# A three-stage kernel on one Trainium2 core: the float64 weights of its first MoE converted without limits, with two VectorE instructions a tile where there were three

## The chip, the cores and the metric

The kernel runs on one core of one Trainium2 chip. The metric is the device time of one execution in microseconds (us). Five engines work side by side, each through its own queue in order: TensorE (PE, with its weight loads as PEld), VectorE (DVE), ScalarE (ACT), GpSimd (POOL) and SyncE (SP), which here issues the loads and stores to HBM.

## The reference, cut to what matters

Attention over a window of 128 positions feeds a dense layer ("first MoE"), and that feeds a layer of eight experts of which each token takes two. The inputs `moe_w_in` and `moe_w_out` arrive as float64.

```python
attn_out = _attn_ref(q, k, v)                      # B 4, H 8, S 576, D 64
x = attn_out.transpose(0, 2, 1, 3).reshape(B * S, H * D)      # 2304 x 512
h = x @ w_in                                       # float64 512 x 2048
x = (softplus(h) @ w_out).astype(np.float32)       # float64 2048 x 512
out = moe2(x, w_gate, w_noise, noise, w1, w2)      # 8 experts, top 2
```

## The kernel before, in words

**Stages.** Attention goes in 20 units of at most 128 queries, each unit in four pairs of heads. `step_a` takes two pairs at once: it multiplies queries by keys on PE (L339); DVE adds the bias and takes the row minimum (L350); ACT takes the exponential (L356); DVE makes the reciprocal of the sum (`rec`, L361 and L362); POOL multiplies the scores by it (`norm`, L371), in the first four units one pair of the two, the other being ACT's (L368). `step_b` transposes the result on PE (L201), with its evacuation on DVE (L400) or ACT (L398). `step_c` multiplies by the values on PE (L190, `t<-pT,rawv`), and the output goes to SBUF as a high part `xh` (ACT, L430) and a low part `xl` (DVE, L435). The tokens then go through the first MoE in chunks of 256: `mm1` (w_in, softplus) and `mm2` (w_out), each product as three fp32r passes of high and low parts. PE alternates MoE matmuls with attention steps until all attention is done; the expert layer follows.

**The conversion.** The 32 weight tiles of the first MoE (16 of w_in, 16 of w_out, 128x512 float64 each) are made into a high and a low fp32r part by `w_convert(i)`, a chain of ten steps: SP loads the 512 KB as pairs of 32-bit words (`load`, L483); ACT reads the high word as a float and takes its absolute value (`first`, L487); ACT scales the low word to an integer (`third`, L491); DVE makes the bits of a float32 out of the high word (`bits`, L495 to L497); POOL adds the low word, in two halves (`whole`, L502); ACT rounds the high part (`high`, L506); DVE, or for some later tiles POOL, subtracts the low part (`low`, L511 or L515); SP stores some of the tiles to HBM for later chunks (`store`, L519). The tiles 0 to 11 are converted while the first attention units run, the others later, two or so for every chunk's turn.

**What sets the order.** The program is written out in order of a plan. `Order` (L25) holds chains of steps with an engine and an assumed cost each, and emits steps in order of assumed time; each engine's queue then runs what it was given, in that order. PE's own order is written by hand (the loop over `t` and the list of attention pieces) and the plan's clock is that of PE's assumed work. `need` and `emitted` force a step's emission before what depends on it. So a changed assumed cost in a chain (the numbers in the call of `chain` at the end of `w_convert`, among them 2.2 us for `bits`) moves steps of other chains on ACT, DVE, POOL and SP. A conversion is started only when fewer than five are in the plan's flight (`convert_some`, NCV = 5). The two DMAs that save the first chunk's `xh` and `xl` (`xspill`, L566) wait on SP until DVE's last L435 of that chunk; loads behind them in SP's queue wait as well.

Of the kernel before, what the change touches and what calls it, by code (L numbers as in the profile page):

```python
# [14 lines left out]
AF = mybir.ActivationFunctionType  # L15
OP = mybir.AluOpType
# [2 lines left out]
P = 128  # L19
BIG = 1.0e30  # L20

F64_LO = 2.0 ** -15
F64_HI = float.fromhex("0x1.a00000p+16")


class Order:
# [11 lines left out]
    def chain(self, *steps, after=0.0):  # L38

        heapq.heappush(self.heap, (self.now + after, self.count, steps, 0))  # L40
        self.count += 1
# [54 lines left out]
def ca(n):  # L96
    return 0.16 + n * 0.00083


def cv(n):  # L100
    return 0.15 + n * 0.00104
# [6 lines left out]
def cg(n):  # L108
    return 0.05 + n * 0.00275
# [3 lines left out]
def moe_chain_kernel(ctx, tc, qk, v, w_in, w_out, w_gate, w_noise, noise, w1, w2, out):  # L113
    nc = tc.nc
    PE, ACT, DVE, POOL, SP = nc.tensor, nc.scalar, nc.vector, nc.gpsimd, nc.sync
# [42 lines left out]
    def f32(ap):  # L158
        return ap.bitcast(F32)
# [3 lines left out]
    def tl(pool, shape, dtype, name, bufs, fin, tag=None, slots=None):  # L163

        r = rings.setdefault(name, [])
        while len(r) >= bufs:
            last = r[-bufs]
            (need if pool is psum else emitted)(last)
            if r[-bufs] == last:
                break  # L170
        r.append(fin)
        return pool.tile(shape, dtype, name=name, tag=tag or name, bufs=slots or bufs)
# [299 lines left out]
    def w_tile():  # L472
        return wpool.tile([P, 2, 512], F32R, name="w", bufs=NRING)
# [3 lines left out]
    def w_convert(i):  # L477
        fc, half = divmod(i, 2)
        d = {}

        def load():
            raw = d["raw"] = wpool.tile([P, 512, 2], I32, name="raw", tag="w", bufs=NRING)
            SP.dma_start(raw.rearrange("p n z -> p (n z)"), (w_out if half else w_in).bitcast(I32)[fc])  # L483

        def first():
            d["a"] = tl(mid, [P, 512], I32, "cva", 4, ("wl", i))
            ACT.activation(f32(d["a"]), f32(d["raw"][:, :, 1]), AF.Abs)  # L487

        def third():
            lo32 = d["raw"][:, :, 0]  # L490
            ACT.activation(lo32, lo32.bitcast(U32), AF.Copy, scale=2.0 ** -29)  # L491

        def bits():
            a = d["a"]
            DVE.tensor_scalar(f32(a), f32(a), F64_LO, F64_HI, op0=OP.max, op1=OP.min)  # L495
            DVE.tensor_scalar(a, a, 3, 0x3FFFFFFF, op0=OP.logical_shift_left, op1=OP.bitwise_and)
            DVE.scalar_tensor_tensor(a, d["raw"][:, :, 1], -0x40000000, a, op0=OP.bitwise_and, op1=OP.bitwise_or)  # L497

        def whole():
            for x in range(2):  # L500
                y = slice(256 * x, 256 * x + 256)
                POOL.tensor_tensor(d["a"][:, y], d["a"][:, y], d["raw"][:, y, 0], OP.add)  # L502

        def high():
            W[i] = w_tile()
            ACT.activation(W[i][:, 0], f32(d["a"]), AF.Copy)  # L506

        def low():
            t = W[i]
            if i < 2 * NA or LOWV[i % len(LOWV)]:  # L510
                DVE.tensor_tensor(t[:, 1], f32(d["a"]), f32(t[:, 0]), OP.subtract)  # L511
            else:
                for x in range(2):
                    y = slice(256 * x, 256 * x + 256)
                    POOL.tensor_tensor(t[:, 1, y], f32(d["a"])[:, y], f32(t[:, 0])[:, y], OP.subtract)  # L515

        def store():
            if i in sidx:
                SP.dma_start(scratch[sidx.index(i)], f32(W.pop(i)).rearrange("p z n -> p (z n)"))  # L519
                nfreed[0] += 1  # L520
        chain(("SP", 0.06, load), ("DMA", (1 << 19) / 330e3, None), (None, 2.0, None),
              ("A", ca(512), first), ("A", ca(512), third), ("V", 2.2, bits),
              ("P", cg(512), whole, ("wa", i)),
              ("A", ca(512), high),
              ("V", cv(512), low, ("wl", i)) if (i < 2 * NA or LOWV[i % len(LOWV)]) else ("P", cg(512), low, ("wl", i)),
              (None, 0.0, lambda: mark_now(("w", i), ("wl", i))),
              ("SP", 0.06, store, ("st", i)))

    def mark_now(key, of):
        o_.done(key, o_.fin[of])  # L530
# [283 lines left out]
    def convert_some():  # L814

        while nconv[0] < due[0] and live1() < room() and (nconv[0] < NCV or ("w", nconv[0] - NCV) in o_.fin):
            w_convert(nconv[0])
            nconv[0] += 1
# [648 lines left out]
```

## Time and profile before

| what | us |
|---|---|
| median of 3 runs | 1135.18 |
| lowest and highest of them | 1135.1, 1136.02 |
| the profiled execution, whole | 1135.73 |
| its span, first to last instruction | 1134.0 |
| PE busy, over the span | 1072.4 |
| DVE busy | 723.6 |
| ACT busy | 616.8 |
| POOL busy | 581.7 |

"Busy" is the time in which an engine had at least one instruction in work. A row of the timeline gives an instruction's start, its duration, engine, line, operation and tiles, and in brackets how long the engine had been idle before it and which instruction released it. A row of the table by stretches gives for each engine the busy time and, in brackets, its instructions; PEclk is the clock that TensorE was granted, as a share of full speed.

### The profile page before, as it was taken

How to read it: one execution, taken by the hardware profiler on the slowest of the kernel's cores; microseconds unless marked ns; L12 is line 12 of the kernel's file. 1: busy time of each engine (PE TensorE's matmuls, PEld its weight loads, DVE VectorE, ACT ScalarE, POOL GpSimd, SP SyncE). 2: the span in 40 equal slices, each digit the busy share in tenths (PEclk: the TensorE clock that was granted, in tenths of full speed). 3: DMA queues.
4: the chain of work that ended last, by engine and by line, in shares of the span. 5: the costliest groups of instructions: out<-in, count | busy, mean ns of one | idle time of the engine just before them, and what ended most of it. 6: DMA issues, size and time to landing. Idle time of an engine off the chain costs nothing.

```text
span 1134.0 us, 21375 instructions
## 1 busy us (share of the span) xinstructions
PE 1072.4 (95%) x7021; PEld 913.2 (81%) x7021; DVE 723.6 (64%) x1946; ACT 616.8 (54%) x1459; POOL 581.7 (51%) x933
## 2 busy tenths in 40 slices
PE   5599999999999999999998997999999999999997
PEld 3377777777789888888887796997997997999984
DVE  8975788889764666666767685653653653665520
ACT  7876768877764444444453543553553553555521
POOL 4576779889886676777775232222222223222112
PEclk8899999999999999999998998999999999999999
DMA  7231553555683322211348729788888888888723
GB/s 306 102 93 57 182 183 118 196 209 176 204 302 124 102 75 75 76 51 62 122 140 304 239 28 337 207 234 262 223 234 264 228 228 253 250 227 233 213 57 38
DMA packets 96561, 198.94 MB, mean 175 GB/s; under 512 B 34048, under 2 KB 44800, under 8 KB 96448
## 3 DMA queue, kind: packets, MB, share of 16 engines
q1 hardware_dynamic: 86112, 176.01, 47.3%
q0 software_dynamic: 10336, 21.54, 9.7%
q8 instruction: 56, 0.92, 0.4%
q14 instruction: 57, 0.47, 0.2%
HBM read 157.82 MB, written 39.69 MB: 174 GB/s over the span
## 4 chain that ended last, share of the span: by engine, by line
PE 65%; DVE 4%; DMA 4%; POOL 3%; ACT 2%; issue 2%; SPq 1%; DVEq 0%; POOLq 0%; ACTq 0%
PE h L190 31%; PE y L190 21%; PE z L190 9%; PE t L201 3%; PE t L190 1%; DMA rawp<-in_moe_w 1%; POOL sl L555 1%; POOL su L555 1%; DVE wlo L1154 1%; DMA rk<-rect 1%; ACT s L356 1%; DMA raw<-in_moe_w_out 1%; DVE gl L587 0%; DMA out<-ys,rc 0%; DMA x1buf<-x 0%
## 5 line engine op out<-in xcount | busy, mean ns | idle before, releaser
L190 PE MATMUL h<-xh,w 128*128 128x256 f32 x1152 | 239.6, 291 | 5.0 <-DVE sl L583 5.0
L1264 POOL DMA_INDIRECT out<-ys,rc x41 | 83.7, 2042 | 272.3 <-DVE ys L1273 131.6
L1154 DVE TENSOR_TENSOR wlo<-rawp,whi 128x1024 fp32r<-128x1024 f32 x107 | 130.8, 1222 | 136.2 <-ACT whi L1156 129.9
L190 PEld LDWEIGHTS h<-xh,w 128*128 128x128 f32 x1152 | 191.2, 193 | 19.2 <-DVE sl L583 9.5
L1156 ACT ACTIVATE whi<-rawp 128x1024 fp32r<-128x1024 f32 x107 | 113.4, 1060 | 151.2 <-PE h L190 108.1
L555 POOL TENSOR_TENSOR su<-sa,su 128x128 f32<-128x128 f32 x288 | 137.2, 497 | 86.1 <-DVE su L588 73.0
L190 PE MATMUL y<-w,gh 128*128 128x512 f32 x552 | 179.8, 407 | 0.0
L190 PE MATMUL h<-xh,whi 128*128 128x256 f32 x576 | 165.5, 287 | 6.4 <-DVE gl L1203 6.4
L190 PE MATMUL h<-xl,w 128*128 128x256 f32 x576 | 164.4, 285 | 1.1 <-DVE xl L435 1.1
L190 PE MATMUL h<-xl,whi 128*128 128x256 f32 x576 | 163.3, 283 | 0.0
L190 PE MATMUL h<-xh,wlo 128*128 128x256 f32 x576 | 163.2, 283 | 0.0
L580 ACT ACTIVATE sa<-h 128x256 f32<-128x256 f32 x144 | 54.8, 381 | 152.7 <-PE h L190 99.6
L555 POOL TENSOR_TENSOR sl<-sl,su 128x128 f32<-128x128 f32 x288 | 134.5, 488 | 3.9 <-DVE sl L583 2.8
L190 PEld LDWEIGHTS h<-xh,whi 128*128 128x128 f32 x576 | 110.1, 191 | 14.0 <-DVE gl L1203 6.8
L190 PEld LDWEIGHTS h<-xl,whi 128*128 128x128 f32 x576 | 110.2, 191 | 7.1 <-issue 1.4
L190 PEld LDWEIGHTS h<-xl,w 128*128 128x128 f32 x576 | 111.4, 193 | 4.5 <-DVE xl L435 1.6
L190 PEld LDWEIGHTS h<-xh,wlo 128*128 128x128 f32 x576 | 110.2, 191 | 0.0
L190 PE MATMUL y<-w,gl 128*128 128x512 f32 x276 | 108.7, 394 | 0.0
L190 PEld LDWEIGHTS y<-w,gh 128*128 128x128 f32 x552 | 95.3, 192 | 16.3 <-issue 2.7
L371 POOL TENSOR_TENSOR s<-s,st 128x256 f32<-128x256 f32 (+2 forms) x144 | 91.9, 661 | 25.6 <-DVE st L362 14.0
L1063 POOL DMA_INDIRECT xg<-x1buf,rc x41 | 43.2, 1054 | 106.6 <-DVE rc L1052 60.4
L587 DVE TENSOR_TENSOR gl<-sl,gh 128x256 fp32r<-128x256 f32 x144 | 76.6, 533 | 13.3 <-ACT gh L585 10.5
(256 smaller groups left out, 2265.0 us busy)
## 6 DMA issues: line engine op xcount, KB each, us to landing
rawp<-in_moe_w SPq DMA_DIRECT2D x140, 512.0 KB
raw<-in_moe_w SPq DMA_DIRECT2D x44, 512.0 KB
qkT<-in_qk SPq DMA_DIRECT2D x20, 512.0 KB
raw<-in_moe_w_in SPq DMA_DIRECT2D x16, 512.0 KB
raw<-in_moe_w_out SPq DMA_DIRECT2D x16, 512.0 KB
out<-zero SPq DMA_DIRECT2D x19, 256.0 KB
xspill<-xh SPq DMA_DIRECT2D x9, 512.0 KB
xspill<-xl SPq DMA_DIRECT2D x9, 512.0 KB
```

What stands on the lines that cost most here:

```text
L190: PE.matmul(o, l, r, start=start, stop=stop)
L201: PE.transpose(o, i, idn)
L356: ACT.activation(s[:nq, j, :n], s[:nq, j, :n], AF.Exp, bias=st[:nq, 0, y], scale=-1.0, accum_out=st[:nq, 1, y])
L371: POOL.tensor_tensor(s[:nq, j, :n], s[:nq, j, :n], st[:nq, 3, 2 * x + j:2 * x + j + 1].to_broadcast([nq, n]), OP.mult)
L555: POOL.tensor_tensor(o[:, z], x[:, z], y[:, z], op)
L580: chain(("A", ca(CT), lambda: ACT.activation(a, ph, AF.Abs)), ("A", ca(CT), lambda: ACT.activation(a, a, AF.Exp, scale=-1.0), ("e", t)), ( ...
L587: ("V", cv(CT), lambda: DVE.tensor_sub(gl, l, f32(gh)), ("g", t)))
L1063: POOL.indirect_dma_start(out=x, out_offset=None, in_=x1buf[:T - 3 * CT if g < NEARLY else TPAD, :], in_offset=bass.IndirectOffsetOnAxis(a ...
L1154: DVE.tensor_sub(lo, t, f32(hi))
L1156: chain(("A", ca(1024), lambda: ACT.activation(hi, t, AF.Copy), None, (("r2", j),)), ("V", cv(1024), low, ("w2", j)))
L1264: POOL.indirect_dma_start(out=out[:, :], out_offset=bass.IndirectOffsetOnAxis(ap=rc[:, a, 0:1], axis=0), in_=ys, in_offset=None, compute_o ...
```

## The change

`first` no longer takes the absolute value of the high word: it multiplies it by 2 to the power -112. `bits` no longer limits the value to a range (the old L495 is gone); the shift to the left by three, which had a mask as its second operation, is a shift alone, and the sign is taken with another mask. The assumed cost of `bits` in the plan goes from 2.2 to 1.6. All else is as it was.

```diff
-F64_LO = 2.0 ** -15
-F64_HI = float.fromhex("0x1.a00000p+16")
...
         def first():
             d["a"] = tl(mid, [P, 512], I32, "cva", 4, ("wl", i))
-            ACT.activation(f32(d["a"]), f32(d["raw"][:, :, 1]), AF.Abs)
+            ACT.activation(f32(d["a"]), f32(d["raw"][:, :, 1]), AF.Copy, scale=2.0 ** -112)
...
         def bits():
             a = d["a"]
-            DVE.tensor_scalar(f32(a), f32(a), F64_LO, F64_HI, op0=OP.max, op1=OP.min)
-            DVE.tensor_scalar(a, a, 3, 0x3FFFFFFF, op0=OP.logical_shift_left, op1=OP.bitwise_and)
-            DVE.scalar_tensor_tensor(a, d["raw"][:, :, 1], -0x40000000, a, op0=OP.bitwise_and, op1=OP.bitwise_or)
+            DVE.tensor_scalar(a, a, 3, None, op0=OP.logical_shift_left)
+            DVE.scalar_tensor_tensor(a, d["raw"][:, :, 1], -0x80000000, a, op0=OP.bitwise_and, op1=OP.bitwise_or)
...
-              ("A", ca(512), first), ("A", ca(512), third), ("V", 2.2, bits),
+              ("A", ca(512), first), ("A", ca(512), third), ("V", 1.6, bits),
```

In the changed program line numbers are lower by two ahead of `bits` and by three behind it: L350 is L348, L361 is L359, L371 is L369, L400 is L398, L435 is L433, L496 and L497 are L493 and L494, L502 is L499, L511 is L508, L555 is L552, L566 is L563, L483 is L481.

DVE, at the second softmax of the second attention unit (`st` is a softmax's statistics, `s` its scores, `cva` a weight tile in conversion), before:

```order
L361 TENSOR_SCALAR st<-st 128x4
L362 RECIPROCAL st<-st 128x4
L400 COPY pT<-y 128x512
L495 TENSOR_SCALAR cva<-cva 128x512
L496 TENSOR_SCALAR cva<-cva 128x512
L497 SCALAR_TENSOR_TENSOR cva<-raw,cva 128x512
L511 TENSOR_TENSOR w<-cva,w 128x512
L495 TENSOR_SCALAR cva<-cva 128x512
L496 TENSOR_SCALAR cva<-cva 128x512
L497 SCALAR_TENSOR_TENSOR cva<-raw,cva 128x512
L350 ISA s,st<-h,relh 128x256
```

and the same place now:

```order
L398 COPY pT<-y 128x512
L359 TENSOR_SCALAR st<-st 128x4
L360 RECIPROCAL st<-st 128x4
L493 TENSOR_SCALAR cva<-cva 128x512
L494 SCALAR_TENSOR_TENSOR cva<-raw,cva 128x512
L348 ISA s,st<-h,relh 128x256
```

Between the reciprocal and the next scores stood two conversions and a subtraction; now one conversion, and the copy of `pT` went ahead of the reciprocal.

POOL, from the first softmax of the second unit on (x2 are two instructions in a row, the two halves of one conversion or the two heads of one norm), before:

```order
L371 TENSOR_TENSOR s<-s,st 128x256 x2
L502 TENSOR_TENSOR cva<-cva,raw 128x256 x2
L371 TENSOR_TENSOR s<-s,st 128x256 x2
L502 TENSOR_TENSOR cva<-cva,raw 128x256 x6
L371 TENSOR_TENSOR s<-s,st 128x256 x2
L502 TENSOR_TENSOR cva<-cva,raw 128x256 x4
L371 TENSOR_TENSOR s<-s,st 128x256 x2
L502 TENSOR_TENSOR cva<-cva,raw 128x256 x4
L555 TENSOR_TENSOR su<-sa,su 128x128 x2
L371 TENSOR_TENSOR s<-s,st 128x256 x2
L555 TENSOR_TENSOR sl<-sl,su 128x128 x2
```

and now:

```order
L369 TENSOR_TENSOR s<-s,st 128x256 x2
L499 TENSOR_TENSOR cva<-cva,raw 128x256 x2
L369 TENSOR_TENSOR s<-s,st 128x256 x2
L499 TENSOR_TENSOR cva<-cva,raw 128x256 x4
L369 TENSOR_TENSOR s<-s,st 128x256 x2
L499 TENSOR_TENSOR cva<-cva,raw 128x256 x2
L369 TENSOR_TENSOR s<-s,st 128x256 x2
L499 TENSOR_TENSOR cva<-cva,raw 128x256 x6
L552 TENSOR_TENSOR su<-sa,su 128x128 x2
L552 TENSOR_TENSOR sl<-sl,su 128x128 x2
L369 TENSOR_TENSOR s<-s,st 128x256 x2
```

One conversion fewer stands ahead of the third norm of this list, two fewer ahead of the fourth, one fewer ahead of the fifth, which now comes behind both halves of the softplus (L552) and not between them.

SP, at the loads of the tiles 5 to 10, before:

```order
L483 DMA raw<-in_moe_w_out 128x1024
L304 DMA qkT<-in_qk 128x1024
L483 DMA raw<-in_moe_w_in 128x1024
L483 DMA raw<-in_moe_w_out 128x1024
L483 DMA raw<-in_moe_w_in 128x1024
L483 DMA raw<-in_moe_w_out 128x1024
L566 DMA xspill<-xh 128x1024
L566 DMA xspill<-xl 128x1024
L483 DMA raw<-in_moe_w_in 128x1024
```

and now:

```order
L302 DMA qkT<-in_qk 128x1024
L481 DMA raw<-in_moe_w_out 128x1024
L481 DMA raw<-in_moe_w_in 128x1024
L481 DMA raw<-in_moe_w_out 128x1024
L481 DMA raw<-in_moe_w_in 128x1024
L563 DMA xspill<-xh 128x1024
L563 DMA xspill<-xl 128x1024
L481 DMA raw<-in_moe_w_out 128x1024
L481 DMA raw<-in_moe_w_in 128x1024
```

The load of tile 5 went behind a load of queries and keys, and that of tile 9 behind the two saves of the first chunk. PE's order is the same in both programs.

## Rows read from the trace of the kernel before

**Rows 1.** Busy time by stretches: us, PE, PEld, DVE, ACT, POOL, PEclk, DMA share, GB/s

```profile
10.00:62.00 52.00, 32.55 (x204) 22.83 (x204) 48.92 (x123) 42.87 (x116) 30.03 (x42) 0.80 0.48 179
62.00:140.00 78.00, 73.19 (x579) 58.73 (x578) 53.56 (x196) 56.83 (x184) 54.19 (x105) 1.00 0.35 114
140.00:330.00 190.00, 181.98 (x1360) 145.51 (x1360) 161.58 (x461) 143.30 (x436) 166.33 (x289) 0.98 0.56 193
```

**Rows 2.** Waits of PE from 10 to 62 us: total us, times, longest us

```profile
PE y L201 <- POOL s L371: 13.3, 4, 5.8
PE t L201 <- POOL s L371: 3.1, 1, 3.1
PE h L339 <- DVE st L350: 2.3, 1, 2.3
```

**Rows 3.** Timeline of all engines, 17.4 to 22 us, around the first long stop

```profile
17.30 0.19 ACT L356 ACTIVATION_READ_ACCUMULATOR s<-s,st 128x1 f32 x1
...
17.43 0.56 DVE L495 TENSOR_SCALAR cva<-cva 128x512 f32<-128x512 f32 x1
...
19.09 0.16 DVE L361 TENSOR_SCALAR st<-st 128x4 f32<-128x4 f32 x1
...
20.88 1.81 POOL L371 TENSOR_TENSOR s<-s,st 128x256 f32<-128x256 f32 x2
...
21.73 0.69 PE L201 MATMUL y<-ident,s 128*128 128x128 f32 x2 [5.83 <-POOL s L371]
```

**Rows 4.** Busy time of line L495 alone, by stretches

```profile
10.00:62.00 52.00, 6.83 (x12) 0.80 0.48 179
140.00:330.00 190.00, 10.15 (x18) 0.98 0.56 193
```

**Rows 5.** The same for L496, then L497, from 10 to 62 us

```profile
10.00:62.00 52.00, 7.54 (x12) 0.80 0.48 179
...
10.00:62.00 52.00, 9.44 (x12) 0.80 0.48 179
```

**Rows 6.** Timeline of all engines, 49.5 to 58.5 us, around the last long stop

```profile
49.75 0.42 DVE L495 TENSOR_SCALAR cva<-cva 128x512 f32<-128x512 f32 x1
...
51.38 0.67 ACT L487 ACTIVATE cva<-raw 128x512 f32<-128x512 f32 x1
...
54.92 1.26 PE L201 MATMUL t<-ident,s 128*128 128x128 f32 x4 [3.14 <-POOL s L371]
```

**Rows 7.** Tile raw: ns of one (min/median/max), first and last start

```profile
L487 ACT ACTIVATE cva<-raw x32: 651/662/683, 10.0 to 320.8; 128x512 f32<-128x512 f32 x32
L491 ACT ACTIVATE raw<-raw x32: 644/668/687, 11.1 to 322.2; 128x512 int32<-128x512 uint32 x32
```

**Rows 8.** Tile cva: ns of one (min/median/max), first and last start

```profile
L502 POOL TENSOR_TENSOR cva<-cva,raw x64: 726/751/1184, 16.3 to 326.7; 128x256 int32<-128x256 int32 x64
...
L495 DVE TENSOR_SCALAR cva<-cva x32: 396/458/962, 14.5 to 323.0; 128x512 f32<-128x512 f32 x32
```

**Rows 9.** Waits of PE from 140 to 330 us

```profile
PE t L190 <- ACT pT L398: 2.3, 1, 2.3
PE t L190 <- DVE st L350: 2.2, 2, 1.4
PE t L201 <- POOL s L371: 1.4, 3, 0.7
```

**Rows 10.** Timeline of PE, 160 to 176 us

```profile
161.57 1.14 PE L339 MATMUL t<-qkT 64*128 64x256 f32 x8
...
168.86 0.44 PE L190 MATMUL t<-pT,rawv 128*64 128x128 f32 x4 [2.33 <-ACT pT L398]
...
171.15 2.08 PE L339 MATMUL t<-qkT 64*128 64x256 f32 x8
```

**Rows 11.** Timeline of SP's DMA issues, 0 to 80 us

```profile
44.67 0.32 SPq L566 DMA_DIRECT2D xspill<-xl  x1
45.05 0.42 SPq L483 DMA_DIRECT2D raw<-in_moe_w_in  x1
```

## The prediction

> **What bounds the kernel now.** First the table of busy time by stretches [rows 1]. From 62 us on PE sets the pace while conversions run: it is busy 73.2 of 78 us and then 182.0 of 190, at a granted clock of 1.00 and 0.98. From 10 to 62 us it is not: PE works 32.6 of 52 us, at a granted clock of 0.80 in the mean, while DVE is busy 48.9 us and ACT 42.9. This stretch, the ramp, holds the first attention units and twelve of the 32 conversions, and the first engine to look at there is DVE.
>
> Second, PE's waits in the ramp [rows 2]: 16.4 us on POOL's norm (13.3 + 3.1) and 2.3 us on DVE's scores, 18.7 us of the 19.4 us that PE is idle. POOL is named, yet POOL is the least loaded engine of the ramp (30.0 us). So, third, the timeline around the longest stop [rows 3] tells why the norm is late: the exponentials of that softmax end at 17.49 us (start and duration of ACT's last read), its reciprocal starts on DVE only at 19.09, because a conversion that begins at 17.43 stands in between; the norm starts at 20.88, and PE goes on at 21.73. DVE's queue is thus the path of the ramp, by way of the softmax.
>
> **The change part by part.**
>
> *One DVE instruction less.* 32 of L495 go. In the ramp there are 12 with 6.83 us together [rows 4], 0.57 us each. Ten of them stand ahead of the reciprocal that ends the last long stop: the tenth starts at 49.75, and PE goes on at 54.92 [rows 6]. Ten times 0.57 is 5.7 us off a queue without gaps.
>
> *The assumed cost.* With 1.6 us for 2.2 the plan puts conversions and softmax steps in another order; PE's order stays. By the order of POOL and DVE, one whole conversion fewer stands ahead of the third norm shown, two ahead of the fourth and one ahead of the fifth. One conversion's other DVE instructions, L496 and L497, are (7.54 + 9.44) / 12 = 1.4 us [rows 5]. That makes 5.7 + 1.4 = 7.1 us less on DVE ahead of the last long stop. What is put off is done after 62 us, where DVE is busy 53.6 of 78 us and PE sets the pace [rows 1]: it costs nothing there. If that cover were gone, the 1.4 us would be back.
>
> *What of the 7.1 us reaches PE.* Not all: the chain also has parts that the change does not touch, namely the exponentials, the norm itself and PE's own work between stops. Bounds: below, only what this one stop shows, where the reciprocal started 1.6 us after its exponentials (19.09 - 17.49); above, the idle time of ACT in the ramp, 52.0 - 42.9 = 9.1 us, since ACT would be full after that. DVE is idle for only 3.1 us of the ramp [rows 1], so most of a shorter queue is a shorter ramp; against it speaks that the copy of `pT`, which waits for PE, now stands ahead of a reciprocal. I take 5.5 us, three quarters of 7.1 and nearer to the queue than to the single stop, and keep 1.6 and 9.1 for the range.
>
> *The other instructions.* The scaled copy that takes the place of the absolute value has its like in L491, a scaled copy at 668 ns beside 662 ns [rows 7]: 32 times 6 ns, 0.2 us on an engine with 9 us to spare, nothing. The shift without its mask and the other mask run over the same tile: nothing; a gain or a loss is bounded by the spread between like instructions, L496 against L495, 7.54 - 6.83 = 0.7 us in the ramp.
>
> *The loads.* Tile 9 is now loaded behind the two saves of the first chunk. Before, the second save was issued at 44.67 and the load right behind it at 45.05 [rows 11]; ACT's conversion of that load's tile began at 51.38 [rows 6], so such a load needs at most 6.3 us. ACT's turn for tile 9 in the new order comes right after the high part of the next attention output (where 51.38 stood before), so the load is hidden, by little. If it were not, ACT's queue with the next exponentials would stand for what is missing; I count 0, and up to 1 us within the lower bound.
>
> *Conversions 12 to 31.* From 140 to 330 us 18 L495 with 10.15 us go [rows 4], and DVE's share falls from 161.6 to some 151 of 190 us. PE's idle time there is only 8.0 us [rows 1], of which 2.2 us wait on DVE's scores and 1.4 us on the norm [rows 9]. The new order may take these away or make others. Above: 3.6 us gained (2.2 + 1.4). Below: one more stop like that at 168.86 costs 2.33 us of waiting, and the clock behind it falls: eight matmuls of L339 took 2.08 us in place of 1.14 [rows 10], so some 3.3 us in all. I take 0, between the two.
>
> *Sum.* 1135.73 - 5.5 = 1130.2 us against the profiled execution. The median of the runs shown, 1135.18, lies 0.55 below that execution, so I predict 1135.18 - 5.5 = 1129.7 us.
>
> **A page against the rows.** L502 on POOL takes 726 to 1184 ns and L495 on DVE 396 to 962 ns [rows 8], so each is stretched at times, where both run. The Trainium skill, page "SBUF — State Buffer", section "Who interferes with whom", says that a VectorE instruction in a two-port mode and a GpSimd instruction lock a shared port for each other, and that the later one stands still until the other is done. By it the removed instruction would also free POOL: 64 times the 25 ns between median and least of L502, an estimate of 1.6 us on POOL, and the time would be 1128.1 if all of it lay on the path. The rows show the stretch, not its cause, and I leave the sum as it is.
>
> **The rivals.**
>
> *The mid-stretch gains too.* The DVE relief also removes PE's waits on scores and norm after 140 us: 5.5 + 3.6 = 9.1 us, 1126.1 us. For it speaks DVE at 85% there; against, POOL at 88% (166.3 of 190), which the change hardly relieves.
>
> *ACT and the chain take over in the ramp.* With DVE's queue shorter, the next thing late is ACT (42.9 of 52 us), whose queue holds three instructions of each conversion between the exponentials; only the 1.6 us of the single stop come through: 1133.6 us. For it: at the first stop ACT ran exponentials and conversions by turns. Against: ACT's 9.1 us of idle time, and the same plan moves ACT's conversion steps back too. That the change does not do what it says, by a dearer scaled copy or shift, would end here as well.
>
> *Slower: POOL's queue after 140 us.* The plan now thinks DVE's part of a conversion 0.6 us shorter and moves POOL's additions (L502, 1.5 us a pair) against norms and softplus steps in a queue that is 88% busy. A norm behind an addition whose input is not there yet stops PE, at 3.3 us a stop as above. Two such stops eat the ramp's 5.5 us; from the third on it is slower. With four: 1129.7 + 13.2 = 1142.9; with three 1139.6, which I take. Against: waits of PE on the norm there are 1.4 us in all now, none above 0.7.
>
> **How the numbers follow.** Forecast, ramp gain between 3 and 8 us: 0.60. Mid-stretch too: 0.14. ACT takes over: 0.14. Slower: 0.12. A measurement of this kernel can tell about 0.2% (2.3 us) from no change. The forecast's own range is 1127.2 to 1132.2. Forecast and first rival are faster by more than 2.3 us: 0.74. The second rival, with 1.6 us, is the same: 0.14. Slower: 0.12. The range for 8 in 10 leaves out the slow rival (0.12) and the far end of the first one (some 0.05), and takes in ACT's case and the upper bound of the ramp (1135.2 - 9.1 = 1126.1) with 1 us of the middle stretch: 1125.0 to 1135.0.
>
> **What would show it right or wrong.** Right: no first VectorE instruction of a conversion; PE's waits on the norm in the ramp fall from 16.4 us to some 11; the matmuls that started at 54.92 start at about 49; the lead of some 5.5 us at 62 us is still there at 330 us and at the end. The second rival would show as ACT without gaps in the ramp and PE's waits as long as before; the slow one as a lead at 140 us that is gone at 330, with new waits of PE on the norm and a granted clock under 0.98 between. What would make the prediction wrong at its root is a ramp whose stops keep their length although DVE has gaps.

## The result, and the profile after

The changed kernel takes 1123.35 us in the median of six executions (1122.71 to 1128.57) beside 1135.14 for the kernel before on the same chip: ratio 0.991, 95% interval 0.9885 to 0.9934. Faster, as forecast, but by about 10 us (10.3 by the ratio) and not by 5.5: the time lies below the range, whose lower end was 1125.0. The profiled execution took 1123.13 us, with a span of 1121.3 (before 1134.0).

Busy time by stretches of the changed kernel, with the columns of [rows 1]:

```profile
10.00:62.00 52.00, 37.02 (x247) 26.10 (x249) 46.02 (x134) 47.26 (x132) 34.79 (x48) 0.84 0.50 182
62.00:140.00 78.00, 75.01 (x589) 60.65 (x588) 54.13 (x188) 56.57 (x186) 56.42 (x109) 1.00 0.34 112
140.00:330.00 190.00, 184.10 (x1382) 149.27 (x1382) 154.05 (x443) 144.60 (x437) 168.22 (x298) 1.00 0.60 208
```

In the ramp PE now works 37.0 of 52 us where it worked 32.6, and DVE has gaps (46.0 for 48.9). PE's waits there, beside [rows 2]:

```profile
PE y L199 <- POOL s L369: 10.2, 4, 5.1
PE t L199 <- ACT cva L485: 2.4, 1, 2.4
PE h L188 <- DVE xl L433: 1.7, 1, 1.7
...
PE t L199 <- POOL s L369: 0.6, 1, 0.6
```

The second row names ACT, but these transposes don't read what ACT's L485 writes. The weight load that goes with them (PEld) names what they do read, POOL's norm:

```profile
49.33 0.20 PEld L199 LDWEIGHTS t<-ident,s 128*128 128x128 f32 x2 [2.64 <-POOL s L369]
```

So the waits on the norm fell from 16.4 to 13.2 us (10.2 + 2.4 + 0.6). The first stop, beside [rows 3], in the timeline of all engines (start, duration, engine, line, operation, tiles):

```profile
17.10 0.42 DVE L493 TENSOR_SCALAR cva<-cva 128x512 int32<-128x512 int32 x1
...
17.29 0.19 ACT L354 ACTIVATION_READ_ACCUMULATOR s<-s,st 128x1 f32 x1
...
18.17 0.16 DVE L359 TENSOR_SCALAR st<-st 128x4 f32<-128x4 f32 x1
...
19.95 1.63 POOL L369 TENSOR_TENSOR s<-s,st 128x256 f32<-128x256 f32 x2
...
21.07 1.26 PE L199 MATMUL y<-ident,s 128*128 128x128 f32 x4 [5.15 <-POOL s L369]
```

The reciprocal starts 0.7 us behind the exponentials (17.48 to 18.17), not 1.6. The last long stop of [rows 6], in PE's timeline, now ends in two pieces:

```profile
49.34 0.44 PE L199 MATMUL t<-ident,s 128*128 128x128 f32 x2 [2.40 <-ACT cva L485]
50.35 0.44 PE L199 MATMUL t<-ident,s 128*128 128x128 f32 x2 [0.58 <-POOL s L369]
```

**The same work, not the same time.** PE has one order in every kernel of this study, so its groups of L339 (L337 after) correspond one to one, and stretches between two such groups hold the same matmuls. The kernel before, by such stretches:

```profile
10.00:64.62 54.62, 35.04 (x228) 24.51 (x228) 51.54 (x135) 45.38 (x122) 31.20 (x43) 0.81 0.46 173
...
140.28:288.92 148.64, 142.71 (x1086) 113.19 (x1085) 130.68 (x391) 116.29 (x364) 130.10 (x230) 0.98 0.52 179
```

and the changed kernel:

```profile
10.00:58.23 48.23, 34.71 (x229) 24.71 (x229) 42.98 (x121) 43.49 (x121) 31.64 (x43) 0.82 0.54 197
...
134.01:277.39 143.38, 139.15 (x1086) 111.21 (x1085) 122.12 (x377) 115.86 (x363) 130.43 (x230) 1.00 0.53 185
```

The ramp won 6.4 us (54.62 - 48.23), nearly all of it idle time of PE (19.6 to 13.5). Half of that is the norm's, 3.2 us; as much, 3.4 us, came from PE's waits on DVE's scores, 2.3 [rows 2] and 1.4 us before, of which 0.3 us is left for the same work, while a wait on `xl` grew by 0.8 us. PE's waits in the ramp, before and after:

```profile
PE t L190 <- DVE st L350: 1.4, 1, 1.4
```

```profile
PE t L188 <- DVE st L348: 0.3, 1, 0.3
```

The middle stretch won another 5.3 (148.64 - 143.38), where the forecast has nothing; of that 1.7 us is idle time (5.9 to 4.2) and 3.6 us is the same 1086 matmuls in less busy time (142.71 to 139.15), at a granted clock of 1.00 for 0.98.

Below, the *lead* of a kernel is the start of such a group in the profile of before, less its start in that kernel's. Times are those of the before column:

| profile | 64.6 us | 161.6 | 181.1 | 288.9 | end of span |
|---|---|---|---|---|---|
| the change | 6.4 | 6.3 | 8.7 | 11.5 | 12.7 |
| after_again (the change) | 4.3 | 4.3 | 3.9 | 5.5 | 8.0 |
| change_again (the change) | 3.7 | 3.6 | 3.8 | 5.3 | 7.7 |
| before_again (before) | 0.0 | 0.1 | -1.5 | -1.5 | -1.7 |
| order_only | 1.5 | 0.8 | 1.5 | 1.6 | 1.6 |
| instr_only | 4.4 | 4.5 | 6.3 | 9.6 | 11.9 |
| ramp_only | 5.4 | 5.3 | 6.3 | 5.6 | 5.1 |
| ramp_instr | 4.0 | 4.1 | 5.4 | 4.7 | 4.4 |
| late_only | -1.7 | -1.4 | -1.3 | 1.7 | 3.2 |
| late_instr | -0.2 | -0.1 | 1.4 | 3.8 | 5.0 |
| four | -5.4 | -5.4 | -5.1 | -11.3 | -14.8 |
| cost19 | 4.6 | 4.7 | 3.7 | 6.7 | 9.2 |
| cost12 | 5.0 | 1.8 | -0.2 | 3.4 | 2.8 |
| flight4 | 6.2 | 1.6 | 2.2 | 5.2 | 4.9 |
| rect_before | -0.5 | -0.3 | 2.2 | 1.1 | 0.8 |
| rect_after | 5.5 | 5.4 | 9.9 | 12.8 | 15.4 |
| rect_instr | 4.4 | 4.5 | 8.7 | 10.8 | 11.9 |

### The profile page after: what moved, and what is told of

It is laid out like the page before. It is cut to its first block, busy times and chain, and to the rows that moved or that the text cites. A ratio compares the mean times of both kernels' runs of the same rounds, so it can differ in the third digit from the quotient of the medians.

```text
span 1121.3 us, 21346 instructions
## 1 busy us (share of the span) xinstructions
PE 1068.9 (95%) x7021; PEld 911.8 (81%) x7021; DVE 705.5 (63%) x1914; ACT 615.0 (55%) x1459; POOL 577.5 (52%) x933
## 4 chain that ended last, share of the span: by engine, by line
PE 67%; DVE 3%; POOL 3%; DMA 3%; issue 2%; ACT 2%; SPq 1%; DVEq 0%; POOLq 0%; ACTq 0%
PE h L188 32%; PE y L188 21%; PE z L188 9%; PE t L199 3%; PE t L188 2%; DMA rawp<-in_moe_w 1%; POOL sl L552 1%; POOL su L552 1%; DVE wlo L1151 1%; DMA rk<-rect 1%; PE t L337 1%; DMA xg<-x1buf,rc 1%; DVE su L585 0%; ACT s L354 0%; POOL cva L499 0%
## 5 line engine op out<-in xcount | busy, mean ns | idle before, releaser
L1261 POOL DMA_INDIRECT out<-ys,rc x41 | 80.9, 1973 | 280.2 <-DVE ys L1270 131.8
L552 POOL TENSOR_TENSOR su<-sa,su 128x128 f32<-128x128 f32 x288 | 135.3, 491 | 84.2 <-DVE su L585 70.9
L552 POOL TENSOR_TENSOR sl<-sl,su 128x128 f32<-128x128 f32 x288 | 136.2, 494 | 4.2 <-DVE sl L580 3.0
L369 POOL TENSOR_TENSOR s<-s,st 128x256 f32<-128x256 f32 (+2 forms) x144 | 92.6, 665 | 30.0 <-DVE st L360 15.6
L585 DVE TENSOR_SCALAR su<-sa 128x256 f32<-128x256 f32 x144 | 64.6, 449 | 34.7 <-ACT sa L578 33.0
```

What stands on the lines that cost most here:

```text
L369: POOL.tensor_tensor(s[:nq, j, :n], s[:nq, j, :n], st[:nq, 3, 2 * x + j:2 * x + j + 1].to_broadcast([nq, n]), OP.mult)
L552: POOL.tensor_tensor(o[:, z], x[:, z], y[:, z], op)
L585: chain(("V", cv2(CT), lambda: DVE.tensor_scalar(u, a, 1.0, 1.0, op0=OP.add, op1=OP.subtract), None, (("e", t),)), ("P", cg(CT), lambda: b ...
L1261: POOL.indirect_dma_start(out=out[:, :], out_offset=bass.IndirectOffsetOnAxis(ap=rc[:, a, 0:1], axis=0), in_=ys, in_offset=None, compute_o ...
```

## The experiments

**Instruction or order.** The change has two halves: the instructions, and the plan's cost, which moves the order. Each alone, and then both for the tiles 0 to 11 (the ramp) or 12 to 31 alone.

order_only is the kernel before with

```diff
-              ("A", ca(512), first), ("A", ca(512), third), ("V", 2.2, bits),
+              ("A", ca(512), first), ("A", ca(512), third), ("V", 1.6, bits),
```

> The kernel before with the plan's cost of bits at 1.6 us, all three VectorE instructions kept. Queue theory (the removed instruction is the cause): the kernel runs within 2 us of before, 1133 to 1137 us, and the lead of TensorE over before at the end of the ramp (62 us) is under 1.5 us. Order theory (the new order puts conversions out of the softmax's way, and that is the cause): 1127 to 1130 us, with a lead of 3 us or more at the end of the ramp.

Measured: 1137.26 us, ratio 1.0012 (1.0002 to 1.0023). The new order alone wins nothing; it is 1.4 us slower by the ratio (0.2 to 2.6), a little above what the queue theory expected.

instr_only has the new instructions and the old cost:

```diff
-            ACT.activation(f32(d["a"]), f32(d["raw"][:, :, 1]), AF.Abs)
+            ACT.activation(f32(d["a"]), f32(d["raw"][:, :, 1]), AF.Copy, scale=2.0 ** -112)
...
-            DVE.tensor_scalar(f32(a), f32(a), F64_LO, F64_HI, op0=OP.max, op1=OP.min)
-            DVE.tensor_scalar(a, a, 3, 0x3FFFFFFF, op0=OP.logical_shift_left, op1=OP.bitwise_and)
...
+            DVE.tensor_scalar(a, a, 3, None, op0=OP.logical_shift_left)
```

> The change with the plan's cost of bits left at 2.2 us, so that the order stays that of before without the first of three instructions. Queue theory: 1123 to 1127 us, with a lead of 5 us or more at the end of the ramp. Order theory: 1131 to 1135 us, with a lead under 3 us at the end of the ramp.

Measured: 1124.69 us, ratio 0.9908 (0.9893 to 0.9923), the same as the whole change within the intervals. With these two orders the instruction is the gain, in the ramp and behind it.

ramp_only and late_only take the change for a part of the tiles (old code and cost for the others):

```diff
+            if i < 2 * NA:
+                ACT.activation(f32(d["a"]), f32(d["raw"][:, :, 1]), AF.Copy, scale=2.0 ** -112)
+            else:
+                ACT.activation(f32(d["a"]), f32(d["raw"][:, :, 1]), AF.Abs)
...
+              ("A", ca(512), first), ("A", ca(512), third), ("V", 1.6 if i < 2 * NA else 2.2, bits),
```

(late_only with `i >= 2 * NA` in both places).

> The change for the tiles 0 to 11 alone; tiles 12 to 31 are converted as before, with 2.2 in the plan. If the two stretches add up, the lead of 6.3 us at 62 us is kept and nothing is won after it: 1128 to 1130 us. Rival: the stops after 140 us depend on how the whole order falls, not on their own instructions, and go with the ramp's change: 1123 to 1126 us.

> The change for the tiles 12 to 31 alone; tiles 0 to 11 as before. If the two stretches add up: no lead at 140 us, some 5 us at 300 us, 1128 to 1131 us. Rival (the later stops go with the whole order): no lead worth naming, 1133 to 1137 us.

Measured: ramp_only 1130.66 us, 0.9955 (0.9942 to 0.9969); late_only 1132.95 us, 0.9981 (0.9968 to 0.9993). Both are slower than what was expected if the two stretches add up (1128 to 1130 and 1128 to 1131); late_only lies at the edge of its rival's range, whose reason the next pair tests. late_only enters its middle stretch 1.4 us behind. Its costs are not the reason: in its trace each engine has the instructions and the order of before up to 120 us, so those 1.4 us are a difference between executions. But its costs do move the order behind that, so the two were run again with the plan's cost left at 2.2 everywhere (ramp_instr, late_instr: the same two conditions on the instructions, no edit of the cost).

> Two VectorE instructions for the tiles 0 to 11, three for the others, the plan's cost 2.2 everywhere, so the order is that of before. Sum theory (with the order fixed, the ramp and the later stretch add up to the 10.4 us of the change with the old order): a lead of 4 to 5 us at 140 us that does not grow, 1130 to 1132 us. Rival (a ramp that ends sooner already frees the later stops): 1124 to 1128 us.

> Two VectorE instructions for the tiles 12 to 31, three for the others, the plan's cost 2.2 everywhere. Sum theory: no lead at 140 us, 4 to 6 us at the end, 1129 to 1132 us. Rival (the later stops do not depend on VectorE's load there): within 2 us of before.

Measured: ramp_instr 1130.4 us, 0.995 (0.9935 to 0.9964); late_instr 1131.78 us, 0.9966 (0.9953 to 0.9978). Against 1134.89 for before that is 5.7 and 3.9 us by the ratios; together 9.6, where instr_only won 10.4 of 1135.2. So the parts add up, and the twenty late tiles are worth about 4 us. Of the middle stretch, ramp_instr has

```profile
136.15:284.21 148.06, 142.56 (x1086) 113.14 (x1085) 129.41 (x391) 116.33 (x365) 130.45 (x230) 0.98 0.51 179
```

and late_instr

```profile
140.36:285.16 144.80, 140.94 (x1086) 112.22 (x1085) 123.06 (x377) 115.76 (x363) 129.03 (x228) 0.99 0.53 183
```

With the late tiles unaltered the stretch keeps its 148 us (its stop on `pT` is shorter, 0.94 us for 2.33, but one on `xl` of DVE follows, 1.70 us, with eight matmuls of L339 at 1.63 us behind it); with them lighter by one instruction it takes 144.8, and 1.6 of those 3.3 us are again busy time of the same matmuls (142.56 to 140.94).

**The mirror.** four runs the instruction that limits the value to a range (L495) twice:

```diff
             DVE.tensor_scalar(f32(a), f32(a), F64_LO, F64_HI, op0=OP.max, op1=OP.min)
+            DVE.tensor_scalar(f32(a), f32(a), F64_LO, F64_HI, op0=OP.max, op1=OP.min)
```

> The kernel before with the first VectorE instruction of bits issued twice (four instructions a tile), the order as before. If VectorE's queue bounds the ramp and its load makes the later stops, the mirror of the change: a lag of 4 us or more at the end of the ramp, 1140 us or more. Rival (the removal opened one slot, a further instruction is absorbed by other waits): under 1138 us.

Measured: 1150.49 us, ratio 1.0124 (1.0103 to 1.0144). PE's waits from 140 to 330 us:

```profile
PE t L201 <- POOL s L371: 5.3, 8, 1.6
PE t L190 <- DVE st L350: 2.0, 1, 2.0
PE t L201 <- DVE xl L435: 1.9, 2, 1.3
```

Its ramp loses 5.4 us and its middle stretch 5.9 (5.4 to 11.3): the same two places as the gain, and another 3.5 us behind them, as the gain has too. The norm that was no stop above 0.7 us [rows 9] now waits up to 1.6.

**The two kernels once more, for a second profile of each**, unaltered:

> The kernel before once more, for a second profile. If the later gain (140 to 290 us) belongs to the change, TensorE's busy time over the same matmuls there is 142 to 144 us again and the stretch lasts 148 to 149 us. Rival (the clock after a stop is a matter of the single execution): TensorE busy 139 to 141 us, and a stretch shorter by 2 us or more.

> The changed kernel once more, for a second profile. If the later gain belongs to the change: TensorE busy about 139 us over the same matmuls, a stretch of 143 to 144 us. Rival (a matter of the single execution): 142 us or more and a stretch of 146 us or more.

Measured, one execution each: 1137.47 and 1127.83 us. The table shows what one profile hides: the change's ramp led by 4.3 us here and not by 6.4, and its middle stretch won 1.2 and not 5.3. Its middle stretch, by the columns of [rows 1], was

```profile
136.00:283.46 147.46, 142.03 (x1085) 113.44 (x1084) 121.47 (x377) 115.76 (x363) 130.39 (x230) 0.98 0.52 180
```

The expected 143 to 144 us with 139 us of work did not come; the rival's sign came, 146 us or more with 142 or more. So a good part of the 5.3 us of the first profile belongs to that execution. That the late tiles win something stands by the timed runs of late_instr, not by that profile.

**The plan's cost.** cost12 and cost19 are instr_only with 1.2 and 1.9 in place of 2.2; flight4 is the change with four conversions in flight where five were:

```diff
-        while nconv[0] < due[0] and live1() < room() and (nconv[0] < NCV or ("w", nconv[0] - NCV) in o_.fin):
+        while nconv[0] < due[0] and live1() < room() and (nconv[0] < 4 or ("w", nconv[0] - 4) in o_.fin):
```

> The change with 1.2 us as the plan's cost of bits, near what the two instructions take without waits. Queue theory (the order matters little): 1122 to 1127 us, as the change. Order theory: a further 3 us or more either way.

> The change with 1.9 us as the plan's cost of bits. If a plan that takes a conversion for dearer than it is keeps conversions out of the softmax's way: 1122 to 1126 us, like 1.6 and 2.2. If the time depends on the single order without a rule: anything between 1122 and 1135 us, as 1.2 gave 1135.

> The change with at most four conversions in the plan's flight in place of five, so that conversions of the ramp are put off further. If conversions in the ramp's queues are what holds the softmax: a lead at the end of the ramp of 7 us or more over before, 1120 to 1124 us. Rival (what is put off comes back between 62 and 140 us or starves the first MoE tiles): no gain over the change, 1124 us or more.

Measured: cost12 1135.21 us, 0.9993 (0.9982 to 1.0003); cost19 1127.07 us, 0.9928 (0.9915 to 0.9941); flight4 1129.09 us, 0.9941 (0.9924 to 0.9957). cost12, expected at 1122 to 1127 if the order matters little, shows that an order can eat the whole gain. It leads by 5.0 us at 64.6 and by 1.8 at 72.7; between them, in its PE timeline:

```profile
64.03 0.30 PE L201 MATMUL t<-ident,s 64*64 64x64 f32 x2 [2.69 <-POOL s L371]
65.05 0.31 PE L201 MATMUL t<-ident,s 64*64 64x64 f32 x2 [0.71 <-POOL s L371]
```

The norm of the short unit of 64 queries is late; flight4 has the same stop and falls from 6.2 to 1.7 there, so its expected lead of 7 us or more was missed. Costs of 1.2, 1.6, 1.9 and 2.2 gave ratios of 0.9993, 0.9909, 0.9928 and 0.9908: the intervals of the last three overlap, and 1.2 alone stands apart.

**What varies in the middle stretch.** In every profile so far PE stops once at about 160 to 174 us on a copy of `pT` by ACT, as in [rows 10]. In the kernel before, the timeline of all engines shows what that copy stands behind (SPq is SP's queue of DMA issues):

```profile
159.92 1.81 SPq L266 DMA_DIRECT2D rect<-pad  x4
161.77 0.84 SPq L483 DMA_DIRECT2D raw<-in_moe_w_in  x1
...
167.61 0.66 ACT L487 ACTIVATE cva<-raw 128x512 f32<-128x512 f32 x1 [3.99 <-DMA raw<-in_moe_w_in]
...
168.43 0.38 ACT L398 ACTIVATE pT<-t 128x256 f32<-128x256 f32 x1
```

and SP's waits from 155 to 163 us why that load was so late:

```profile
SPq L266 <- DVE pad L263: 10.9, 1, 10.9
```

Four writes of a table (`prepare1`, L259 to L266) hold SP until DVE has made their tile; the weight load behind them is issued at 161.77, its conversion holds ACT idle for 3.99 us, and the copy that PE wants is behind it. Three kernels move those four writes, and nothing else, behind the next two weight loads; the order of the other engines is unaltered. rect_before is the kernel before, rect_after the change, rect_instr instr_only, each with

```diff
+        return pad
+
+    def prepare1b(pad):
         for r in rect:
             SP.dma_start(r.rearrange("(p n) z -> p (n z)", p=P), pad.rearrange("p n z -> p (n z)"))
...
         if t == 20:
-            prepare1()
+            pad1 = prepare1()
+        if t == 24:
+            prepare1b(pad1)
```

and change_again is the change, unaltered, on the same chip.

> The kernel before, with four DMAs moved in SP's order alone: the writes of `pad` to `rect` go behind the next two weight loads (all other engines keep their order). In the profile of before SP stands 10.9 us on these writes, the weight load behind them is issued at 161.77, ACT stands 3.99 us on that load, and PE stops for 2.33 us on a `pT` copy queued behind it on ACT, with eight matmuls at 2.08 us for 1.14 after it. Theory (the stop is made by the late load, and the low clock by the stop): ACT's wait on the load and PE's stop at about 168.9 go, the eight matmuls take 1.14, and PE leads before by 2.5 to 3.5 us at 182 us; whole time 1131.5 to 1133.5. Rival (the stop is DVE's and ACT's own load of work): ACT's wait goes, PE stops all the same within the next unit, time within 1 us of before.

> The change, with the same four DMAs moved. The two profiles of the change stop there for 1.90 and 3.19 us, the second with eight matmuls at 1.84 us behind it and 4.7 us more in all. Theory (the length of this stop, set by when the load lands, is what makes executions of the change differ): the stop goes in each execution, the runs no longer fall into two groups 5 us apart, and the median is 1119.5 to 1122. Rival (the executions differ for other reasons, the ramp's among them): runs still spread over 5 us, median 1121.5 to 1125.5.

> The change itself once more, unaltered, on the same chip as the others: 1123 to 1128 us, ratio 0.989 to 0.994, runs near 1123 or near 1128. If its executions differ by the stop on ACT's copy at some 162 us, a profile of a run near 1123 shows that stop under 2.1 us with eight matmuls of 1.13 behind it, and one near 1128 a longer stop with matmuls above 1.6 us.

> Two instructions with the old plan cost of 2.2 us, and the four DMAs moved. With the old cost the stop there was 1.05 us with no lower clock behind it, so less is to be had: 1122 to 1124.5 by the theory, which counts the stop alone; 1124 to 1126 (as without the move) by the rival.

Measured: rect_before 1134.76 us, 0.9991 (0.998 to 1.0002); rect_after 1120.01 us, 0.9862 (0.984 to 0.9883); change_again 1125.6 us, 0.9902 (0.9885 to 0.992), five runs from 1123.65 to 1128.03; rect_instr 1124.14 us, 0.9897 (0.9876 to 0.9918). In rect_after SP issues that load at 144.11:

```profile
144.11 0.37 SPq L484 DMA_DIRECT2D raw<-in_moe_w_in  x1
...
158.94 2.49 SPq L267 DMA_DIRECT2D rect<-pad  x4
```

and PE has neither the stop nor slow matmuls behind it:

```profile
156.20 1.13 PE L340 MATMUL t<-qkT 64*128 64x256 f32 x8
162.94 1.13 PE L340 MATMUL t<-qkT 64*128 64x256 f32 x8
171.22 1.13 PE L340 MATMUL t<-qkT 64*128 64x256 f32 x8
```

In the profile of change_again (an execution of 1128.03 us) stop and slow matmuls are there, if at 1.45 us and not above the 1.6 expected; first ACT, then PE:

```profile
163.17 0.66 ACT L485 ACTIVATE cva<-raw 128x512 f32<-128x512 f32 x1 [4.38 <-DMA raw<-in_moe_w_in]
```

```profile
165.49 0.44 PE L188 MATMUL t<-pT,rawv 128*64 128x128 f32 x4 [2.57 <-ACT pT L396]
168.67 1.45 PE L337 MATMUL t<-qkT 64*128 64x256 f32 x8
```

What follows. The stop is the late load's: with the load early it is gone in all three kernels. What that is worth in time differs. rect_before won 2.6 us there (-0.34 to 2.24 at 181 us), but its whole time, forecast at 1131.5 to 1133.5, was missed: half of the lead is lost again at a stop that lasted 0.48 us in before,

```profile
197.42 0.78 PE L201 MATMUL t<-ident,s 128*128 128x128 f32 x4 [1.64 <-DVE xl L438]
```

where by this row DVE is the next thing late (the weight load of these transposes names POOL's norm, which here waits for DVE's reciprocal). In rect_after, with two instructions a conversion, the lead is kept, and it comes to 1120.01 us, faster than both kernels; its interval lies below that of change_again on the same chip, by little (4.5 us between the two ratios). rect_instr can't be told from instr_only. So one kernel of the three shows a gain in whole time. The second theory on trial, that this stop alone makes executions of the change differ, had its number in rect_after (four runs within 2.7 us) and fell on the rest: six runs of rect_instr, without the stop, spread from 1122.22 to 1128.27 us; the timed executions of the change spread from 1122.7 to 1128.6 us with some at 1125.5 to 1125.9 in between, where two groups were expected; and its three profiles differ by 2.7 us before they reach the stop.

## Why the prediction was right and wrong

**The ramp: right.** Forecast 5.5 us of a possible 7.1, from a single profile. Three profiles of the change lead by 6.3, 4.3 and 3.6 at 161.6 us: 4.7 in the mean. More profiles bear on it, since ramp_only and rect_after have the change's program up to 120 us, and late_only, late_instr and rect_before that of before: at 64.6 us the five of the one lead the five of the other by 5.5 us in the mean. That the size fits so well is luck in part, for the three quarters of 7.1 were chosen between two bounds, and single profiles of one program lie up to 2.7 us apart. The reasoning by the queue is not luck: the mirror loses 5.4 us in the same place. Its two pieces were not of one worth: the instruction alone won 4.5 (instr_only) and 4.1 us (ramp_instr), the order alone 0.8, and the whole of order_only is no faster. Of the signs named, the matmuls of 54.92 came at 49.34 in the profiled execution, but the norm waits fell by 3.2 us, to 13.2, where 5.4 less, some 11, was named. The prediction followed DVE's queue by way of the norm alone; half of the ramp's gain came by way of the scores, which DVE makes itself. instr_only has most of its gain there, with norm waits of

```profile
PE y L201 <- POOL s L371: 12.5, 5, 5.2
PE t L201 <- POOL s L371: 2.7, 1, 2.7
```

and 0.8 us left of the 3.7 on scores; the sign was weaker than it was made out.

**The other instructions and the loads: right.** The scaled copy L485 takes no longer than the absolute value did, beside [rows 7]; the new shift is as long as the old one, 6.59 us for 11 beside 7.54 for 12 [rows 5]. Tile 9's load, issued at 40.09, was in time: ACT begins on it at 46.56, and from 10 to 62 us ACT waits for no load. Tile cva, ns of one (min/median/max):

```profile
L499 POOL TENSOR_TENSOR cva<-cva,raw x64: 724/740/1299, 15.8 to 315.1; 128x256 int32<-128x256 int32 x64
L485 ACT ACTIVATE cva<-raw x32: 646/658/673, 10.0 to 310.1; 128x512 f32<-128x512 f32 x32
```

POOL was not relieved either: for the same work of the middle stretch it is busy 130.10 us before and 130.43 after. The Trainium skill, page "SBUF — State Buffer", section "Who interferes with whom", by whose lock an estimate of 1.6 us on POOL would have come free, is not borne out in that size: the 64 additions (L502) took 50.7 us before and 50.6 in instr_only, where the instruction is gone and the order kept. The three profiles of the change have 49.8, 49.3 and 49.3 us, but order_only, which keeps the instruction, has 49.8 as well. Leaving it out of the sum was right.

**Conversions 12 to 31, "I take 0": wrong.** This is the step that failed: by late_instr the late tiles are worth 3.9 us (2.5 to 5.3). It has two faults.

First, the ceiling. It was set at 3.6 us from PE's *waits* [rows 9]; the price of the slower clock behind a stop was worked out in the same paragraph, 3.3 us for a stop of 2.33, and booked on the side of the loss alone. A stop that gets shorter gives that back as well. In the profiled execution 3.6 of the 5.3 us won are busy time of the same matmuls. And the waits that the ceiling did count, on scores and norm, mostly stayed: 2.8 us for this work before (1.4 of the norm and 1.4 of the 2.2 on scores [rows 9]), 2.2 after, by PE's waits from 134.01 to 277.39 us:

```profile
PE t L188 <- ACT pT L396: 1.9, 1, 1.9
PE t L199 <- POOL s L369: 1.2, 2, 0.7
PE t L188 <- DVE st L348: 1.0, 1, 1.0
```

The place is [rows 10] itself; after, in PE's timeline:

```profile
155.30 1.13 PE L337 MATMUL t<-qkT 64*128 64x256 f32 x8
...
162.16 0.44 PE L188 MATMUL t<-pT,rawv 128*64 128x128 f32 x4 [1.90 <-ACT pT L396]
...
164.15 1.13 PE L337 MATMUL t<-qkT 64*128 64x256 f32 x8
```

The stop is 0.4 us shorter, the eight matmuls behind it take 1.13 us for 2.08, and the lead grows from 6.3 to 8.7.

Second, the stretch was looked up on a list of PE's waits and not followed back. The largest stop (2.3 us on `pT`) begins with SP's 10.9 us of standing; a weight load's landing sets its length, and that makes it differ from execution to execution: 1.90, 3.19 and 2.57 us for the change, 2.33 and 2.79 for before. What DVE's relief gives without it is steadier: from 188.7 to 288.9 us the three profiles of the change gain 2.9, 1.6 and 1.5 us, of which 1.1 us in each is less waiting (`xl` 0.5, scores 0.4, norm 0.2) and the rest the same matmuls in less time.

**After 289 us: not counted.** The three profiles of the change gain another 1.2, 2.5 and 2.4 us there. Two waits of PE on a softplus of DVE became shorter by 0.8 us (0.81 and 0.49 us before, 0.31 and 0.19 in the change's first profile). But most of the gain lies past 600 us, where no conversion runs any more. The same 348 matmuls behind one stop, in before and in change_again:

```profile
601.48:659.94 58.46, 55.50 (x348) 48.88 (x349) 41.02 (x128) 25.91 (x48) 24.33 (x28) 0.95 0.80 261
```

```profile
595.85:652.55 56.70, 54.24 (x348) 48.17 (x349) 41.34 (x128) 26.25 (x48) 24.89 (x29) 0.97 0.82 268
```

They take 59.23 us in before_again, 56.67 in after_again, but 58.20 in the change's first profile; the stop ahead of them lasts 3.74 or 3.75 us in all five. So 1.7 of the 2.1 us that the sum below has for this stretch come with a difference in granted clock behind the same stop, and why the executions differ there is open.

**The sum.** Mean lead of the three profiles of the change over the mean of the two of before, in us: ramp 4.7, middle stretch 2.7 + 0.8 = 3.5, behind it 2.0 + 0.1 = 2.1; together 10.3, and the ratio says 10.3 of 1135.14. So the forecast named the largest piece and priced it well; the other half is the two stretches that it put at nothing. The rival "the mid-stretch gains too" (1126.1, given 0.14) was the better account: DVE's relief does reach that stretch, and its 3.6 us are near the 3.5 found. But the size is luck, for the waits that it counted on fell by 0.6 us in the profiled execution, and it too has nothing behind 289 us.

**The other rivals.** ACT did not take over, though it is near: 47.3 of 52 us busy. The slow one, a norm late on POOL, did not come with a cost of 1.6 us; cost12 and flight4 show that it was a real case, in another place (64 to 72 us, not after 140) and dearer by the stop: 3.1 and 4.5 us of lead.

## What to carry to other kernels

Price a stop of PE with the matmuls behind it, on the side of the gain as on that of the loss: compare the same matmuls in both profiles, not only the waits. Follow each stop on the list back to its queue, over engines, before the stretch is put at nothing; here the chain ran from DVE over SP's queue, a load and ACT to PE, and one reordering of four DMA issues was worth 4.5 us by the ratios with the changed kernel, but nothing that could be told with two others (1134.76 and 1124.14 us), one of which stopped for longer at the next thing late. And take a plan's assumed cost as part of the change, with its own run: it moved the time by some 10 us with the same instructions (ratios of 0.9993 and 0.9908). And take more than one profile before a few us are put down to a place.

## What was not expected of the hardware

How much the stops cost beyond their length. PE's order being one, the time from the end of the `pT` stop to the end of the next eight matmuls of L339 is for the same work in every profile: 3.12 us after stops of 1.05, 1.39 and 1.90 us (instr_only, late_instr, the change), 4.66 after one of 2.09 (order_only), 4.37 and 5.56 after 2.33 and 2.79 (before, before_again), 4.63 and 4.66 after 2.57 and 3.19 (change_again, after_again). The other seven profiles with this stop agree: 3.12 us after 0.94, 1.05 and 1.10, and 4.34 to 5.56 after 2.19, 2.75, 2.77 and 3.47. The granted clock shows it: from the stop on, the kernel before has

```profile
168.86:176.00 7.14, 7.14 (x42) 5.46 (x44) 6.01 (x19) 6.01 (x19) 5.95 (x11) 0.76 0.24 95
```

and the change, over as long a stretch,

```profile
162.16:169.30 7.14, 7.13 (x55) 5.81 (x56) 5.64 (x18) 6.49 (x24) 6.36 (x12) 1.00 0.16 67
```

42 matmuls against 55 in the same 7.14 us, both without a gap: the first ran for a part of it at the lower of the clock's two levels (1.2 of 2.4 GHz, 0.76 in the mean), the second all through at the upper one. So a difference of 0.43 us in waiting went with one of some 2 us in the work behind it.

The other surprise is the spread inside the ramp: the three profiles of the change lead by 6.4, 4.3 and 3.7 us at 64.6 us with one order on every engine, and late_only, with the program of before up to there, is 1.7 us behind before; no run was made that tells why. Those of instr_only and rect_instr have the same lead there to 0.01 us.
